# Sums on VectorE, output weights' splits two places ahead, operands kept by operand and loaded in place

## The chip, the cores and the metric

The kernel runs on one core of a Trainium2 chip. The metric is the device time of one execution in microseconds. A core has five engines with queues of their own, each working in order: TensorE (PE, matmuls), VectorE (DVE), ScalarE (ACT), GpSimd (POOL) and SyncE (SP, which here only issues DMAs). DMAs move data between device memory and on-chip memory; matmuls add into banks of their own, from which VectorE and ScalarE take the results. A queue that waits holds up everything behind it on its engine.

## The reference

With S = 2048 tokens, D = 1024, 32 heads of 32 and F = 3584, all in fp32:

```python
q, k, v = layernorm(x) @ wqkv            # phi(t) = (t + 1 if t > 0 else exp(t)) + 1e-6
kv  = sum over tokens of phi(k) v        # per head, 32 x 32
den = phi(q) . (sum of phi(k)) + 1e-6
s = ((phi(q) kv) / den) @ wo
g = silu((silu(xn @ w1) * (xn @ w3)) @ w2)      # xn = layernorm(x)
return x + s * g
```

## The kernel before

Each fp32 operand is split into a high and a low part (`split`, L79: ScalarE casts to the high part, VectorE subtracts it for the low one), and each product is three matmuls (`mm3`, L89: high x high, high x low, low x high). Large products are done by a scheme with seven block products in place of eight: the left side is used as A11, S2, S3, S1, A12, A22, S4 and the right side as B11, T2, T3, T1, B21, T4, B22, where the S and the T are sums and differences of blocks. `four_sums` (L591) makes S1 to S4 of a left operand, `sums_of` (L627) the T of a right one; both work on GpSimd.

The stages follow each other on TensorE: layernorm and transposes of x; then two halves of the tokens, each with products for k, v and q and 14 pairs of gate and up (products named like `ag`, `cu`, `du`); then the attention's output product (Segment "s", eight token groups m); then five layers B0 to B4, which multiply the hidden values with slices of w2 and add into `acc`; the last of them ends in `finish` (L1007: silu, times s, added to the output by an accumulating DMA).

Beside the pairs of a half run side jobs. `catch_up` takes one step of the first job at each block product (12 matmuls in a half): in half 0 the preparation of half 1 and the sums of w2 (`weight_sums`, L635), in half 1, in this order, denominators, `merge_wo` (L755), `divide` (L725), again denominators and divide. A job's `yield True` ends a step. Steps that are left at a half's end are run one after the other. The order of instructions on each engine is set by a scheduler with a timeline of its own, within the program's dependencies.

`merge_wo(k)` multiplies the masked kv of heads (`kvm`) with rows of wo, split as `wos`; the bank `wp` of the product is copied back over wo, and the sums of the four results are stored to `wp_d` as the attention's right operands. `divide(m, k)` loads phi(q) and the reciprocals r of a token group into a tile `qd`, multiplies, makes the four sums in it and stores it to `qs_d`. Its tiles come from a ring of three, `job_tile`, which all jobs share, and from which group 0 of the attention takes the raw tiles of its left operands too (`r0q_0`, `r2q_0`, `r4q_0`, `r6q_0`).

`use_up` (L613) stores the hidden values to `h_d` and `sums` (L619) their sums to `hs_d`; `left` (L957) reads the parts of the left operands from them, for the layers (`hiddens`) as for the attention (`queries`, from `qs_d`). A raw tile is loaded and then split into a tile X of pool `pb`. The attention's right operands are loaded as `wpr` into a ring of two (`attention_right`, L1051) and split into `wp`, which lies where the left operands of half 1 were: wp0 over A11, wp1 over S2, wp2 over S3, wp3 over S1, wp4 over A12, wp5 over A22, wp6 over S4.

Of the kernel before, what the change touches and what calls it, by code (L numbers as in the profile page):

```python
# [22 lines left out]
def tile_linear_attention_times_swiglu(  # L23
# [37 lines left out]
    nc.vector.memset(zacc, 0.0)  # L61

# [17 lines left out]
    def split(pair, src, bias=None):  # L80

        hi, lo = pair[:, 0], pair[:, 1]
        if bias is None:
            nc.scalar.copy(out=hi, in_=src)  # L84
            return nc.vector.tensor_sub(out=lo, in0=src, in1=hi.bitcast(F32))
# [505 lines left out]
    def four_sums(x1, x2, s12, s34):  # L591
# [3 lines left out]
        s1, s2 = (s12.rearrange("p (n g s) -> p n g s", n=2, s=P)[:, n] for n in range(2))  # L595
        s3, s4 = (s34.rearrange("p (n g s) -> p n g s", n=2, s=P)[:, n] for n in range(2))
        nc.gpsimd.tensor_add(out=s1, in0=a21, in1=a22)  # L597
# [3 lines left out]
        nc.gpsimd.tensor_sub(out=s4, in0=a12, in1=s2)  # L601
        yield

    def hidden(h, pair):
# [22 lines left out]
    def sums_of(b11, b12, b21, b22):  # L627

        nc.gpsimd.tensor_sub(out=b11, in0=b12, in1=b11)  # L629
# [99 lines left out]
    def divide(m, k):  # L729
# [13 lines left out]
        def steps(t):  # L743
# [5 lines left out]
            nc.gpsimd.dma_start(out=qs_d[m][:, k], in_=t)  # L749
# [5 lines left out]
    def merge_wo(k):  # L755
# [9 lines left out]
        def steps(e, t):  # L765
# [5 lines left out]
            split(kvm, f)  # L771
            for n in range(2):
# [339 lines left out]
```

## Time and profile before

| | before |
|---|---|
| runs | 2426.34, 2426.35, 2428.03 us; median 2426.35 |
| span of the profiled execution | 2428.0 us |
| TensorE busy | 2350.3 us, 97 % |
| VectorE busy | 1785.2 us, 74 % |
| ScalarE busy | 933.7 us, 38 % |
| GpSimd busy | 611.7 us, 25 % |
| DMA | 425.40 MB, mean 175 GB/s |

The profiled execution's own time is known only by its span, 2428.0 us; the slowest of the three runs took 2428.03. A busy TensorE is not TensorE at its peak: a matmul of 128x512 may follow another sooner than its recorded duration, so the count of matmuls in a stretch tells more than its busy time. In lists of waits stand the waiting engine, what it wrote and its line, what released it, and the total in us, the times and the longest. In tables by stretch stand, for each engine, the busy us and the number of instructions, then TensorE's granted clock, the DMA engines' busy share and GB/s. In groups of instructions stand line, engine, operation, written and read names, shape and count, then busy us and the mean ns of one, or three durations (least, median, most).

### The profile page before, as it was taken

What the parts mean: (1) busy time and instruction counts of PE and PEld (TensorE: products, weight loads), DVE (VectorE), ACT (ScalarE), POOL (GpSimd) and SP (SyncE); (2) the same over time, 40 slices, a digit from 0 to 9 for tenths busy, and PEclk for the clock granted to TensorE, in tenths of its full rate; (3) what the DMA queues carried; (4) which work ended last, traced back from release to release, by engine and by line L of the source; (5) the groups of instructions that cost most, each with busy time, mean ns of one, the idle gap of its engine ahead of it and who ended that gap; (6) DMA issues with size and microseconds to landing.
All of it is one profiled execution on the core that took longest, in us unless ns stands there. A gap on an engine that the chain in (4) does not pass through costs nothing.

```text
span 2428.0 us, 30795 instructions
## 1 busy us (share of the span) xinstructions
PE 2350.3 (97%) x10544; PEld 1937.2 (80%) x10544; DVE 1785.2 (74%) x2699; ACT 933.7 (38%) x1659; POOL 611.7 (25%) x848
## 2 busy tenths in 40 slices
PE   7999999999999999999889999999899999999997
PEld 5788888788888888887767888888687788888876
DVE  8655888888887765567777878887655576766786
ACT  4434544333333244354333333334323533342432
POOL 3000112356756210010333544243330000000032
PEclk9999999999999999999999999999899999999999
DMA  3211455567667641134454555457776565876698
GB/s 123 85 52 62 148 166 170 177 210 239 224 203 238 238 174 53 53 113 129 139 186 165 199 184 197 146 183 238 247 231 196 173 206 160 258 236 181 197 232 199
DMA packets 380285, 425.40 MB, mean 175 GB/s; under 512 B 20528, under 2 KB 309296, under 8 KB 380016
## 3 DMA queue, kind: packets, MB, share of 16 engines
q1 hardware_dynamic: 349600, 327.74, 43.2%
q0 software_dynamic: 30528, 95.70, 11.9%
q8 instruction: 82, 1.34, 0.2%
q14 instruction: 75, 0.61, 0.1%
HBM read 277.35 MB, written 153.35 MB: 177 GB/s over the span
## 4 chain that ended last, share of the span: by engine, by line
PE 78%; DMA 7%; DVE 7%; issue 4%; POOL 2%; ACT 1%; SPq 0%; POOLq 0%; DVEq 0%; ACTq 0%
PE cB L92 1%; PE kv L507 1%; DMA wpr<-wp_d 1%; PE dB L94 1%; PE cB L94 1%; PE dB L92 1%; PE cB L93 1%; PE dB L93 1%; PE aB L92 1%; PE aB L94 1%; PE aB L93 1%; DMA rA12B<-h_d 1%; PE den L714 1%; DVE acc L879 1%; PE trk L474 1%
## 5 line engine op out<-in xcount | busy, mean ns | idle before, releaser
L615 POOL DMA_DIRECT2D h_d<-sg x112 | 61.6, 550 | 359.2 <-DVE sg L614 354.8
L576 POOL DMA_DIRECT2D pq_d<-pq x32 | 17.4, 545 | 481.1 <-DVE pq L468 481.0
L896 POOL DMA_DIRECT2D u_d<-uB x32 | 17.3, 540 | 415.6 <-DVE uB L879 343.3
L879 DVE TENSOR_TENSOR acc<-cB,acc 128x512 f32<-128x512 f32 x50 | 34.4, 689 | 38.8 <-PE cB L94 38.8
L597 POOL TENSOR_TENSOR qd<-qd 128x128 f32<-128x128 f32 x32 | 25.2, 788 | 145.6 <-DVE qd L746 132.5
L879 DVE TENSOR_TENSOR acc<-dB,acc 128x512 f32<-128x512 f32 x56 | 38.6, 689 | 27.7 <-PE dB L94 27.5
L601 POOL TENSOR_TENSOR hs<-sg,hs 128x256 f32<-128x256 f32 x56 | 52.4, 935 | 1.6
L598 POOL TENSOR_TENSOR hs<-hs,sg 128x256 f32<-128x256 f32 x56 | 48.2, 860 | 0.0
L629 POOL TENSOR_TENSOR w<-w 128x256 f32<-128x256 f32 x28 | 26.0, 930 | 70.4 <-DMA w<-in_B_w 70.4
L600 POOL TENSOR_TENSOR hs<-sg 128x256 f32<-128x256 f32 x56 | 43.7, 781 | 0.0
L597 POOL TENSOR_TENSOR hs<-sg,sg 128x256 f32<-128x256 f32 x56 | 43.0, 768 | 1.0
L1020 POOL DMA_DIRECT2D out<-acc x28 | 24.3, 879 | 66.3 <-DVE acc L1015 61.5
L1002 POOL DMA_DIRECT2D s_d<-s x32 | 17.4, 544 | 93.5 <-DVE s L879 46.1
L84 ACT CAST XS4B<-rS4B 128x384 fp32r<-128x384 f32 (+1 forms) x40 | 19.7, 492 | 53.5 <-PE cB L94 37.4
L84 ACT CAST XA11B<-rA11B 128x384 fp32r<-128x384 f32 (+1 forms) x40 | 19.7, 492 | 50.0 <-PE dB L94 21.2
L92 PE MATMUL aB<-B,XA12B 128*128 128x512 f32 x87 | 35.2, 404 | 3.5 <-ACT XS2B L84 3.2
L92 PE MATMUL cB<-T,XA22B 128*128 128x512 f32 x87 | 34.9, 401 | 3.6 <-DVE acc L879 3.3
L84 ACT CAST XA12B<-rA12B 128x384 fp32r<-128x384 f32 (+1 forms) x40 | 19.7, 493 | 48.1 <-PE dB L94 22.5
L84 ACT CAST XA22B<-rA22B 128x384 fp32r<-128x384 f32 (+1 forms) x40 | 19.7, 492 | 43.5 <-PE aB L94 25.0
L92 PE MATMUL aB<-B,XA11B 128*128 128x512 f32 x87 | 34.2, 393 | 1.5 <-ACT XA11B L84 1.5
L84 ACT CAST XS3B<-rS3B 128x384 fp32r<-128x384 f32 (+1 forms) x40 | 19.7, 493 | 41.1 <-DMA rS3B<-hs_d 18.5
L507 PEld LDWEIGHTS kv<-kvr 128*128 128x128 f32 x256 | 33.5, 191 | 2.5
(5846 smaller groups left out, 8759.5 us busy)
## 6 DMA issues: line engine op xcount, KB each, us to landing
h_d<-sg POOLq DMA_DIRECT2D x112, 256.0 KB, 3.4
qs_d<-qd POOLq DMA_DIRECT2D x32, 512.0 KB, 3.7
hs_d<-hs POOLq DMA_DIRECT2D x60, 256.0 KB, 4.1
w<-in_B_w SPq DMA_DIRECT2D x56, 256.0 KB
wt_d<-w SPq DMA_DIRECT2D x28, 512.0 KB
hs_d<-hs SPq DMA_DIRECT2D x52, 256.0 KB
pq_d<-pq POOLq DMA_DIRECT2D x32, 256.0 KB, 3.2
a_dS<-xo SPq DMA_DIRECT2D x16, 512.0 KB
```

What stands on the lines that cost most here:

```text
L84: nc.scalar.copy(out=hi, in_=src)
L92: nc.tensor.matmul(acc, lhsT=wh, rhs=ah, start=start, stop=False, skip_group_check=True)
L93: nc.tensor.matmul(acc, lhsT=wh, rhs=al, start=False, stop=False, skip_group_check=True)
L94: nc.tensor.matmul(acc, lhsT=wl, rhs=ah, start=False, stop=stop, skip_group_check=True)
L507: nc.tensor.matmul(acc, lhsT=r[:, 1, t], rhs=r[:, 0, t], start=t == 0, stop=t == C // P - 1)
L597: nc.gpsimd.tensor_add(out=s1, in0=a21, in1=a22)
L598: nc.gpsimd.tensor_sub(out=s2, in0=s1, in1=a11)
L600: nc.gpsimd.tensor_sub(out=s3, in0=a11, in1=a21)
L601: nc.gpsimd.tensor_sub(out=s4, in0=a12, in1=s2)
L615: nc.gpsimd.dma_start(out=h_d[i][2 * h + c][:, 2 * k + n], in_=sg[n, c])
L629: nc.gpsimd.tensor_sub(out=b11, in0=b12, in1=b11)
L879: return V.tensor_add(out=c, in0=src, in1=c)
```

## The change

- `four_sums` and `sums_of` work on VectorE.
- `merge_wo` splits both halves of wo, and lets a step pass, before it multiplies them; the steps of a job grow from 3 to 5 (first of a pair) and from 7 to 10 (second). Its stores go through POOL's queue.
- The hidden values and their sums go to one tensor `ho_d`, kept by operand: all that one left operand needs of a token group lies together for each partition. A21 is not stored. `qs_d` is kept by operand too.
- The layers' left operands, and wp2 to wp6, are loaded into the low half of their split tile and split in place. The left operands of groups 1 to 7 of the attention come into the two large raw tiles.
- Pools `pb`, `pe`, `pc` end with the attention; the layers have pools of their own: `px` with 12 split left operands, `pl`, `pd`, `pu` and two for `acc`.

```diff
-    h_d = [[dram.tile([P, f1 - f0, C], F32, name=f"h_d{f0}_{c}") for c in range(NCH)] for f0, f1 in FB]
-    hs_d = [[dram.tile([P, (f1 - f0) // 2, 2, C], F32, name=f"hs_d{f0}_{c}") for c in range(NCH)] for f0, f1 in FB]
+    KEPT = ["A11", "A12", "A22", "S1", "S2", "S3", "S4"]
+    ho_d = [[dram.tile([P, NT, len(KEPT), (f1 - f0) // 2, P], F32, name=f"ho_d{f0}_{c}") for c in range(NCH)]
+            for f0, f1 in FB]
...
-    qs_d = [dram.tile([P, ND // 2, 4, 2 * P], F32, name=f"qs_d{m}") for m in range(S // (2 * P))]
+    QUERIES = ["A11", "A21", "A12", "A22", "S1", "S2", "S3", "S4"]
+    qs_d = [dram.tile([P, len(QUERIES), ND // 2, P], F32, name=f"qs_d{m}") for m in range(S // (2 * P))]
...
-    def split(pair, src, bias=None):
+    def split(pair, src=None, bias=None):
 
         hi, lo = pair[:, 0], pair[:, 1]
+        if src is None:
+            src = lo.bitcast(F32)
...
-    pb = ctx.enter_context(tc.tile_pool(name="pb", bufs=8))
-    pe = ctx.enter_context(tc.tile_pool(name="pe", bufs=3))
-    pc = ctx.enter_context(tc.tile_pool(name="pc", bufs=6))
     era1 = ExitStack()
+    pb = era1.enter_context(tc.tile_pool(name="pb", bufs=8))
+    pe = era1.enter_context(tc.tile_pool(name="pe", bufs=3))
+    pc = era1.enter_context(tc.tile_pool(name="pc", bufs=6))
...
-        s1, s2 = (s12.rearrange("p (n g s) -> p n g s", n=2, s=P)[:, n] for n in range(2))
-        s3, s4 = (s34.rearrange("p (n g s) -> p n g s", n=2, s=P)[:, n] for n in range(2))
-        nc.gpsimd.tensor_add(out=s1, in0=a21, in1=a22)
-        nc.gpsimd.tensor_sub(out=s2, in0=s1, in1=a11)
+        s1, s2 = (s12.rearrange("p (g n s) -> p g n s", n=2, s=P)[:, :, n] for n in range(2))
+        s3, s4 = (s34.rearrange("p (g n s) -> p g n s", n=2, s=P)[:, :, n] for n in range(2))
+        nc.vector.tensor_add(out=s1, in0=a21, in1=a22)
+        nc.vector.tensor_sub(out=s2, in0=s1, in1=a11)
         yield
-        nc.gpsimd.tensor_sub(out=s3, in0=a11, in1=a21)
-        nc.gpsimd.tensor_sub(out=s4, in0=a12, in1=s2)
+        nc.vector.tensor_sub(out=s3, in0=a11, in1=a21)
+        nc.vector.tensor_sub(out=s4, in0=a12, in1=s2)
...
-            nc.gpsimd.dma_start(out=h_d[i][2 * h + c][:, 2 * k + n], in_=sg[n, c])
+            halves = sg[n, c].rearrange("p (g t s) -> p g t s", t=2, s=P)
+            if n == 0:
+                nc.gpsimd.dma_start(out=ho_d[i][2 * h + c][:, :, 0, k], in_=halves[:, :, 0])
+            else:
+                nc.gpsimd.dma_start(out=ho_d[i][2 * h + c][:, :, 1:3, k], in_=halves)
...
-                queue.dma_start(out=hs_d[i][2 * h + c][:, k, e], in_=o[e])
+                queue.dma_start(out=ho_d[i][2 * h + c][:, :, 3 + 2 * e:5 + 2 * e, k],
+                                in_=o[e].rearrange("p (g n s) -> p g n s", n=2, s=P))
...
-        nc.gpsimd.tensor_sub(out=b11, in0=b12, in1=b11)
-        nc.gpsimd.tensor_sub(out=b12, in0=b22, in1=b12)
+        nc.vector.tensor_sub(out=b11, in0=b12, in1=b11)
+        nc.vector.tensor_sub(out=b12, in0=b22, in1=b12)
         yield True
-        nc.gpsimd.tensor_sub(out=b22, in0=b22, in1=b11)
-        nc.gpsimd.tensor_sub(out=b21, in0=b21, in1=b22)
+        nc.vector.tensor_sub(out=b22, in0=b22, in1=b11)
+        nc.vector.tensor_sub(out=b21, in0=b21, in1=b22)
...
-            nc.gpsimd.dma_start(out=qs_d[m][:, k], in_=t)
+            nc.gpsimd.dma_start(out=qs_d[m][:, :, k], in_=t.rearrange("p a (n s) -> p (a n) s", s=P))
...
+            o = [pb.tile([P, 2, C], FR, tag="b", name=f"wos{j}_{n}") for n in range(2)]
             for n in range(2):
-                o = pb.tile([P, 2, C], FR, tag="b", name=f"wos{j}_{n}")
-                split(o, t[:, n])
+                split(o[n], t[:, n])
                 yield True
+            yield True
+            for n in range(2):
                 acc = bank(f"wp{j}_{n}")
-                mm3(acc, (kvm[:, 0], kvm[:, 1]), (o[:, 0], o[:, 1]), True, True)
+                mm3(acc, (kvm[:, 0], kvm[:, 1]), (o[n][:, 0], o[n][:, 1]), True, True)
                 nc.scalar.copy(out=t[:, n], in_=acc)
-            yield True
+                yield True
             if e:
                 b = [t[:, n] for t in both for n in range(2)]
                 for n, i in (("B11", 0), ("B21", 2), ("B22", 3)):
                     store(n, b[i])
+                yield True
                 yield from sums_of(*b)
+                yield True
                 for n, i in (("T1", 0), ("T3", 1), ("T4", 2), ("T2", 3)):
                     store(n, b[i])
-                for _ in range(3):
+                for _ in range(2):
                     yield True
 
         def store(n, t):
             g, e = divmod(7 * k + PRODUCTS.index(n), 4)
-            nc.sync.dma_start(out=wp_d[g][:, e], in_=t)
+            nc.gpsimd.dma_start(out=wp_d[g][:, e], in_=t)
...
+        staged = None
+        for e, n in enumerate(PRODUCTS):
+            n = PARTNER[n]
+            if e % (2 if m == 0 else 4) == 0:
+                staged = (job_tile([P, 2, ND // 2, P], f"r{e}q_{m}") if m == 0 else
+                          praw.tile([P, 4, ND // 2, P], F32, tag="raw", name=f"r{e}q_{m}"))
+            raw = staged[:, e % (2 if m == 0 else 4)]
+            loads[:] = [nc.sync.dma_start(out=raw, in_=qs_d[m][:, QUERIES.index(n)])]
+            yield n, pb.tile([P, 2, ND // 2, P], FR, tag="b", name=f"X{n}q_{m}"), raw
...
-        h_ = h_d[i][m // NT].rearrange("p (k e) s -> p k e s", e=2)
-        hs = hs_d[i][m // NT]
-        return left(m, m % NT, [h_[:, :, e] for e in range(2)], [hs[:, :, e] for e in range(2)],
-                    (FB[i][1] - FB[i][0]) // 2, f"B{i}")
+        for n in PRODUCTS:
+            n = PARTNER[n]
+            t = px.tile([P, 2, (FB[i][1] - FB[i][0]) // 2, P], FR, tag="x", name=f"X{n}B{i}_{m}")
+            loads[:] = [nc.sync.dma_start(out=t[:, 1].bitcast(F32), in_=ho_d[i][m // NT][:, m % NT, KEPT.index(n)])]
+            yield n, t, None
...
-            raw = praw.tile([P, 4, C], F32, tag="raw", name=f"wpr{g}")
+            place = pa.tile([P, 4, 2, C], FR, tag=AOPS[g], name=f"wp{g}")
+            raw = praw.tile([P, 4, C], F32, tag="raw", name=f"wpr{g}") if g < 2 else None
             for i in range(2):
-                nc.sync.dma_start(out=raw[:, 2 * i:2 * i + 2], in_=wp_d[g][:, 2 * i:2 * i + 2])
-            places[g] = raw, pa.tile([P, 4, 2, C], FR, tag=AOPS[g], name=f"wp{g}")
-        return places[g][0][:, e]
+                o = slice(2 * i, 2 * i + 2)
+                nc.sync.dma_start(out=place[:, o, 1].bitcast(F32) if raw is None else raw[:, o], in_=wp_d[g][:, o])
+            places[g] = raw, place
+        return places[g][0] if places[g][0] is None else places[g][0][:, e]
...
-    pw = ctx.enter_context(tc.tile_pool(name="pw", bufs=1, reuse_waits="tile"))
+
+    def late_pool(name, bufs=1):
+        return ctx.enter_context(tc.tile_pool(name=name, bufs=bufs, reuse_waits="tile"))
+
+    pu, pacc, pl, pw, pacc2, pd, px = (late_pool(*how) for how in (
+        ("pu", 3), ("pacc",), ("pl", 6), ("pw",), ("pacc2",), ("pd", 2), ("px", 12)))
+
+    def late_small(name):
+        pool, tag = (pd, "d") if name.startswith("xs") else (pl, "c")
+        return pool.tile([P, C], F32, tag=tag, name=name)
```

ScalarE's queue at the first pair of merge_wo, before (`wos` the split wo, `kvm` the masked kv, `wp` the bank of their product, the others operands of hidden products):

```order
807 L84 CAST wos_0_9344<-wo_9243 128x512
808 L84 CAST kvm_9341<-kvf_9339 128x128
809 L84 CAST T3g_1__9365<-wg_1__9151 128x512
810 L778 COPY wo_9243<-wp_0_9368 128x512
811 L84 CAST wos_1_9373<-wo_9243 128x512
812 L84 CAST B21g_1__9390<-wg_1__9151 128x512
813 L84 CAST T2g_1__9363<-wg_1__9151 128x512
814 L778 COPY wo_9243<-wp_1_9393 128x512
815 L84 CAST kvm_9420<-kvf_9418 128x128
816 L84 CAST wos_0_9423<-wo_9337 128x512
817 L84 CAST T4g_1__9441<-wg_1__9151 128x512
818 L778 COPY wo_9337<-wp_0_9444 128x512
```

And now:

```order
806 L90 CAST kvm_9323<-kvf_9321 128x128
807 L90 CAST T1g_1__9311<-wg_1__9133 128x512
808 L90 CAST wos_0_9326<-wo_9225 128x512
809 L90 CAST T3g_1__9348<-wg_1__9133 128x512
810 L90 CAST wos_1_9327<-wo_9225 128x512
811 L90 CAST B21g_1__9367<-wg_1__9133 128x512
812 L791 COPY wo_9225<-wp_0_9388 128x512
813 L90 CAST T2g_1__9346<-wg_1__9133 128x512
814 L414 COPY ug_1__9483<-ag_1__9484 128x512
815 L90 CAST T4g_1__9408<-wg_1__9133 128x512
816 L90 CAST B22g_1__9440<-wg_1__9133 128x512
817 L791 COPY wo_9225<-wp_1_9411 128x512
```

The cast of wos_1 stood behind the copy of wp_0, the product of wos_0; now both casts stand ahead of it, and two operands of other products with them.

SP's queue around the end of the hidden products, before (`qd5_3` is the last of the jobs ahead of the attention, `r0q_0` to `r6q_0` the left operands of its group 0, `wpr` its right operands):

```order
L740 DMA qd5_3_13487<-pq_d1_2_82 128x256
...
L973 DMA r0q_0_13697<-qs_d0_145 128x4x128 x2
L1056 DMA wpr1_13741<-wp_d1_125 128x1024 x2
L973 DMA r2q_0_13706<-qs_d0_145 128x4x128 x2
L973 DMA r4q_0_13715<-qs_d0_145 128x4x128 x2
L1056 DMA wpr2_13753<-wp_d2_126 128x1024 x2
L1056 DMA wpr3_13765<-wp_d3_127 128x1024 x2
L973 DMA r6q_0_13724<-qs_d0_145 128x4x128
L1056 DMA wpr4_13777<-wp_d4_128 128x1024 x2
```

And now, where `wp6` waits for the last hidden product, each qd for the store of the tile before it in the ring, and r0q_0 for that of qd5_1:

```order
L751 DMA qd5_0_13581<-pq_d1_2_84 128x256
L1062 DMA wp6_13779<-wp_d6_112 128x2x512 x2
L749 DMA qd5_1_13640<-r_d2_137 128x1x256
...
L749 DMA qd5_2_13651<-r_d2_137 128x1x256
...
L749 DMA qd5_3_13662<-r_d2_137 128x1x256
...
L751 DMA qd5_3_13662<-pq_d1_2_84 128x256
L982 DMA r0q_0_13679<-qs_d0_127 128x512 x2
L982 DMA r2q_0_13688<-qs_d0_127 128x512 x2
L982 DMA r4q_0_13697<-qs_d0_127 128x512 x2
L982 DMA r6q_0_13706<-qs_d0_127 128x512
```

The left operands of group 0 stood among the loads of wpr, behind qd5_3 as the last job; now they stand behind all of wp and behind qd5_1 to qd5_3, which themselves come after wp6.

More of the change, by code (lines that the diff above doesn't have):

```diff
@@ L834, in tile_linear_attention_times_swiglu, with __init__ @@
     class Segment:
-        def __init__(self, name, nk, first, last, place, right, left, acc, end=None):
-            self.last, self.U = last, {}
+        def __init__(self, name, nk, first, last, place, right, left, acc, sum_of, end=None):
+            self.last, self.U, self.sum_of = last, {}, sum_of
             self.name, self.nk, self.first = name, nk, first
@@ L955, in tile_linear_attention_times_swiglu @@
     loads = []
-    def left(m, g, halves, sums, nk, name, first=False):
-        halves = [t.rearrange("p k (g t s) -> p k g t s", t=2, s=P) for t in halves]
-        sums = [t.rearrange("p k (n g s) -> p k n g s", n=2, s=P) for t in sums]
-        where = {"A11": halves[0][:, :, g, 0], "A12": halves[1][:, :, g, 0], "A22": halves[1][:, :, g, 1]}
-        for n in range(4):
-            where[f"S{n + 1}"] = sums[n // 2][:, :, n % 2, g]
-        big = None
-        for e, n in enumerate(PRODUCTS):
-            n = PARTNER[n]
-            if first:
-                if e % 2 == 0:
-                    big = job_tile([P, 2, nk, P], f"r{e}{name}_{m}")
-                t = big[:, e % 2]
-            else:
-                t = signed(f"r{n}{name}_{m}")[:, :nk * P].rearrange("p (k s) -> p k s", s=P)
-            loads[:] = [nc.sync.dma_start(out=t, in_=where[n])]
-            yield n, t
     def queries(m):
@@ L1045, in run @@
                 around(m)
-            seg.tokens(m, m == 0 or m == NG - 1 and nxt is not None, between)
+            seg.tokens(m, m == 0 or m == NG - 1 and (ends or nxt is not None), between)
     places = {}
@@ L1068, in tile_linear_attention_times_swiglu @@
         attention.right(k)
-    run(attention)
+    run(attention, ends=True)
     assert all(next(j, None) is None for j, _ in jobs)
@@ L1085, in tile_linear_attention_times_swiglu @@
         layers[0].right(k)
[L1086 removed]
+    acc.extend((pacc if m < 5 else pacc2).tile([P, 2, 2, C], F32, tag=f"acc{m}", name=f"acc{m}") for m in range(NG))
     for i, seg in enumerate(layers):
```

27 lines of the change are left out of this document (14 added, 13 removed).

## The prediction

> **What bounds the kernel now.** I read the page first. TensorE is busy nearly all the span, and the chain of work that ended last runs through it for four fifths.
>
> ```profile
> PE 2350.3 (97%) x10544; PEld 1937.2 (80%) x10544; DVE 1785.2 (74%) x2699; ACT 933.7 (38%) x1659; POOL 611.7 (25%) x848
> PE 78%; DMA 7%; DVE 7%; issue 4%; POOL 2%; ACT 1%; SPq 0%; POOLq 0%; DVEq 0%; ACTq 0%
> ```
>
> So time can only be won where TensorE is not at its rate. I find these places by stretches of 100 us: the count of matmuls in brackets behind the first number, the granted clock after the five engines.
>
> ```profile
> 400.00:500.00 100.00, 97.98 (x441) 80.50 (x440) 83.09 (x121) 42.44 (x73) 23.04 (x34) 0.98 0.51 162
> 500.00:600.00 100.00, 100.00 (x443) 82.81 (x442) 90.64 (x102) 33.80 (x57) 68.23 (x86) 1.00 0.70 230
> 1100.00:1200.00 100.00, 90.13 (x379) 71.87 (x379) 73.71 (x99) 41.97 (x75) 18.73 (x24) 0.97 0.41 134
> 1200.00:1300.00 100.00, 90.49 (x377) 71.64 (x376) 76.28 (x93) 35.09 (x65) 32.35 (x35) 0.97 0.47 154
> 1300.00:1400.00 100.00, 100.00 (x443) 82.78 (x442) 83.08 (x104) 32.02 (x54) 48.14 (x75) 1.00 0.57 193
> 1700.00:1800.00 100.00, 91.63 (x381) 72.97 (x380) 59.00 (x85) 29.20 (x50) 32.33 (x57) 0.93 0.78 244
> 1800.00:1900.00 100.00, 92.69 (x390) 73.42 (x389) 54.44 (x94) 37.72 (x76) 17.11 (x31) 0.97 0.64 204
> 2000.00:2100.00 100.00, 98.95 (x436) 81.21 (x435) 68.55 (x120) 35.95 (x68) 3.24 (x6) 1.00 0.64 198
> 2300.00:2400.00 100.00, 92.83 (x383) 73.83 (x382) 79.85 (x132) 34.76 (x69) 34.13 (x33) 0.95 0.93 230
> ```
>
> A full stretch of the wide products holds 443 matmuls, one per 0.2257 us. Matmuls missing from 443 times 0.2257 is what a stretch lost: 14.4 + 14.9 = 29.3 us in 1100 to 1300 (merge_wo), 14.0 in 1700 to 1800 (start of the attention), 12.0 in 1800 to 1900 (its end and the start of layer B0), 1.6 in 2000 to 2100, 13.5 in 2300 to 2400 (last layer); in 400 to 500, 2.0 idle and 0.02 of the clock, together some 3. The waits say on what:
>
> ```profile
> PE wp L92 <- ACT wos L84: 11.5, 8, 4.5
> PE T1s L92 <- ACT wp L84: 5.2, 1, 5.2
> PE cB L92 <- DVE acc L879: 3.3, 1, 3.3
> PE aB L92 <- ACT XS2B L84: 3.2, 2, 2.3
> PE wp L93 <- DVE wos L85: 3.2, 1, 3.2
> PE B11B L92 <- ACT B L84: 2.9, 1, 2.9
> PE wp L92 <- ACT kvm L84: 1.8, 1, 1.8
> ```
>
> **Sums on VectorE.** POOL loses its additions in four_sums and sums_of; VectorE gains them. Prices, GpSimd's and VectorE's on the same or the nearest shape:
>
> ```profile
> L601 POOL TENSOR_TENSOR hs<-sg,hs 128x256 f32<-128x256 f32 x56 | 52.4, 935 | 1.6
> L629 POOL TENSOR_TENSOR w<-w 128x256 f32<-128x256 f32 x28 | 26.0, 930 | 70.4 <-DMA w<-in_B_w 70.4
> L597 POOL TENSOR_TENSOR qd<-qd 128x128 f32<-128x128 f32 x32 | 25.2, 788 | 145.6 <-DVE qd L746 132.5 <-DMA qd<-pq_d 10.5 <-DMA hs_d<-hs 2.6
> L508 DVE TENSOR_TENSOR kvacc<-kv,kvacc 128x128 f32<-128x128 f32 x32 | 9.1, 284 | 0.0
> L85 DVE TENSOR_TENSOR XA11B<-rA11B,XA11B x40: 414/550/1650, 1839.6 to 2396.2; 128x384 fp32r<-128x384 f32 x32, 128x256 fp32r<-128x256 f32 x8
> L321 DVE TENSOR_TENSOR wu__5040<-wu__5040 128x512 f32<-128x512 f32 x4 | 7.7, 1923 | 0.1
> L321 DVE TENSOR_TENSOR wq__1786<-wq__1786 128x512 f32<-128x512 f32 x4 | 2.8, 692 | 0.1
> ```
>
> VectorE gets 56 x 4 hidden sums and 28 x 4 weight sums at 0.414 (its 128x256 price), 32 x 4 query sums at 0.284 and 16 sums of 128x512 at 0.692: 93 + 46 + 36 + 11 = 186 us. It also loses the stretching: the L321 group at 1923 ns ran beside POOL sums, the one at 692 with POOL free of them. In the fullest stretch, 500 to 600, its 102 instructions at an undisturbed 0.68 are 69 us, and the 64 sums that POOL has there add 27: 96 of 100. So VectorE is close to full there but not over it, and TensorE, with no loss there now, should stay so: cost 0, covered by queued products; if that cover is gone, it is what lies above 100. The one stall of the stretched evacuations (400 to 500) goes: **-3** (bounds -3 and 0).
>
> **merge_wo two places ahead.** Before, ScalarE's cast of the second half of wo stands behind the copy of the first product's bank, so each pair waits for itself. Now both casts come ahead of the copy, with 15 to 44 matmuls (3.4 to 9.9 us) between what the split needs and the product that reads it; a cast is 0.62 (as XA11's, below), a split or an evacuation's add 0.69, three or four in a row: under the slack. The waits (11.5 + 3.2 + 1.8 = 16.5) go, and with them most of the clock's share, 0.03 of two stretches, 6 us, and the short refills: of 29.3 I take **-25** (bounds -15, the waits nearly alone, and -29).
>
> VectorE's new wait stands here: sums_of writes over halves of wo whose stores (POOL's queue now) must have landed, 3.4 us as s_d's below, with one place, 2.7, between; four stalls of about 1 us, behind which evacuations queue, covered by the same slack: 0 (up to +3, inside the bounds above). The stores themselves (0.55 us an issue, POOL idle for three quarters), the order of the kept operands in ho_d, and A21 left out of it cost nothing that any wait shows.
>
> **The start of the attention.** merge_wo takes more places than it had (5 for 3 and 10 for 7 in a pair of jobs, 20 more over four pairs, some 54 us at 12 matmuls, 2.7 us, a place), so the division jobs behind it slip: qd4_3 and qd5_0 to qd5_3 now fall after the last hidden product. The left operands of token group 0 use the same three buffers as these jobs, and SP's order shows them behind qd5_3. Before, they were cast at 1673.8, ahead of the last hidden product.
>
> ```profile
> 1680.00:1690.00 10.00, 10.00 (x46) 8.29 (x45) 6.51 (x12) 3.44 (x7) 2.32 (x5) 1.00 0.93 279
> 1690.00:1700.00 10.00, 10.00 (x46) 8.29 (x45) 9.20 (x15) 5.91 (x12) 2.56 (x5) 1.00 0.93 291
> 1710.00:1720.00 10.00, 4.64 (x11) 2.53 (x9) 2.89 (x4) 1.20 (x3) 1.86 (x3) 0.51 0.96 294
> L973 SPq DMA_DIRECT2D r0q<-qs_d x2: 559/590/622, 1670.4 to 1671.0; - x2
> L84 ACT CAST XA11s<-r0q x1: 622/622/622, 1673.8 to 1673.8; 128x512 fp32r<-128x512 f32 x1
> qs_d<-qd POOLq DMA_DIRECT2D x2, 512.0 KB, 5.0
> L738 SPq DMA_DIRECT2D qd<-r_d x64: 517/530/926, 1257.1 to 1796.8; - x64
> L746 DVE SCALAR_TENSOR_TENSOR qd<-qd 128x512 f32<-128x512 f32 x32 | 21.8, 682 | 3.6 <-DMA qd<-pq_d 3.6
> ```
>
> Let T be the end of the last hidden product. VectorE's queue after T, in its order: c12u, three sums, two wp splits, the gate's product, more sums and splits: qd4_3's last sum at T+7, four wp5 splits, qd5_0's product, two wp6 splits and its sums to T+14; its store lands 5.0 later (the landing in this stretch), T+19. Only then qd5_3 may load (four issues of 0.53, landing 3.3 after its issue as r0q did): T+24; product and sums 0.7 + 4 x 0.28: T+26. Beside it qd5_1's last sum, T+18, its store, T+23, r0q_0's load 3.3, T+26.4, cast 0.6: **TensorE at T+27**, if no transfer queues. But they do: from wp4's load (allowed 60 matmuls, 13.5 us, ahead of T) up to r0q_0 there are five loads of wp (5.2 MB), seven of group 1 (1.8), five of qd (2.6), four stores of qs_d (2.1) and the last pair's stores (1.8), 13.5 MB; at the 285 GB/s of the full rows, 47 us: T+34, and T+36 with the cast. I take T+30. The long idle costs a half-clock stretch behind it (the row at 0.51 is one), 3 us. So 33 in place of 14.0: **+19** (bounds: +11, for T+22 at the unloaded landing of 3.7, and +25). The waits for wp (T1s, 5.2) hide under it.
>
> **The start of B0.** The weight loads of B0 go into memory of the closed pools, so the first waits for the last store of s.
>
> ```profile
> s_d<-s POOLq DMA_DIRECT2D x32, 256.0 KB, 3.4
> L990 SPq DMA_DIRECT2D rB11B<-in_B_w x2: 333/442/551, 1857.0 to 1865.1; - x2
> L84 ACT CAST B<-rB11B x1: 617/617/617, 1860.3 to 1860.3; 128x512 fp32r<-128x512 f32 x1
> ```
>
> Before, this load was out at 1857.0, ahead of the attention's end (1858.0: the 2.9 us wait for B ended with this cast). Now: evacuation 0.8, landing 3.4, load 3.3, cast 0.6: 8.1 us for 2.9, +5. Of the 12.0 lost here, 6 are neither this wait nor the clock's 3; the left operands of B0, now loaded far ahead, had a part in them, and I take 1: **+4** (bounds 0, with all 6 gone, and +8, with the store's landing doubled).
>
> **Later layers.** Left operands load in place, 12 tiles deep; before, 4 raw and 8 split tiles gave the same depth, so lookahead is unchanged. What changes is 1,536 contiguous bytes where it was 512, and no stall of the raw ring: some of the 6.5 us of waits in the last layer (cB, aB) and their clock goes, though the DMA at 0.93 stays near full. **-6** (bounds 0 and -12). The small loss at 2000: **-1** (0 to -1.6). The tail with xs loaded earlier: **-2** (0 to -3).
>
> **A rule against it.** The stores of qs_d go out in 1,024 pieces of 512 bytes where they were 128 of 4 KB.
>
> ```profile
> L749 POOL DMA_DIRECT2D qs_d<-qd x32: 531/554/573, 1317.2 to 1816.1; - x32
> ```
>
> By this row an issue is 0.55 us with 128 pieces; nothing here shows one with 1,024. Bounds: 0.55, and eight times that, 4.4. I take the lower, since no row shows a growth. The Trainium skill ("DMA: Bandwidth & Descriptors", section "Anatomy of one DMA") calls descriptor generation small and variable, so that many can be emitted before it shows, which is the first bound; the same page (section "SWDGE vs HWDGE vs iDMA") has GpSimd compute one pair for each piece, which leans to the second and would add three dearer stores to the chain, some +12 in the sum. No run here decides it.
>
> **Sum.** -3 - 25 + 19 + 4 - 6 - 1 - 2 = -14. The profiled execution's span is 2428.0 and the runs have a median of 2426.35, so the difference is set against the median: **2412 us**.
>
> **Rivals.**
> 1. The start does no more harm than before: the transfers before T run ahead, since group 0's operands are ready when the DMA queue is (before it was full too, 0.93 to 0.96). For it: VectorE is only at 0.6 to 0.9 around there, so the sums may come earlier than my count. Against: r0q_0 stands behind four stores in a chain. -33 in all: 2393.
> 2. Slower: the piecewise stores are dear (4.4 us an issue, and the rate of the rows with small pieces, 230 GB/s, in place of 285, so that the 13.5 MB take 59 us, T+46, and the three stores 4 more): TensorE at T+50, +39 at this place. Sum +6, or +12 without the last layer's gain: 2434. It decides from T+44 on, where the gain at merge_wo is eaten.
> 3. The change doesn't do what it says: TensorE still waits in merge_wo, now for wo's load or a late bank; -10 there instead of -25, sum about +1: 2427. Against: the wait named ACT's cast, not a DMA.
>
> **How the numbers follow.** A measurement of this kernel tells about 0.2 %, 5 us, from no change. Chances: the forecast 0.59 (2400 to 2424 with its own bounds), rival 1 0.17, rival 2 0.16, rival 3 0.08. Faster: 0.49 of the forecast, all of rival 1, 0.66; same: 0.08 of the forecast, 0.04 of rival 2, 0.05 of rival 3, 0.17; slower the rest, 0.17. The range takes in most of rival 1 and rival 2's point: 2388 to 2434.
>
> **What would show it.** Right: no "wp <- ACT wos" of some us in the waits; 1100 to 1300 near 440 matmuls a stretch; at the start of the attention one wait of TensorE for the cast of XA11 of group 0, of about 30 us, with r0q loaded last; at B0 a wait of 8; no POOL sums beyond the preparation, and L321 groups at 0.69. Wrong: that wait below 14 us or above 43; VectorE at 100 % with TensorE waiting in 500 to 600; qs_d issues on POOL well over 0.55 us; waits for wos as before.

## The result and the profile after

The changed kernel takes 2446.83 us (median of 4 runs, 2443.98 to 2448.69), the kernel before 2427.19 us in the same comparison: a ratio of 1.0066, 95 % interval 1.0049 to 1.0084. It is slower: the two medians differ by 19.6 us, and the ratio makes it 16 us, between 12 and 20. The forecast was 2412, 14 us faster, in a range from 2388 to 2434; the measured time lies above that range. The profiled execution has a span of 2446.7 us. All medians below are of executions in the usual state; one of e6, 2492.5 us at a lower granted clock, is left out.

First the page of the changed kernel, busy times and the chain that ended last:

```profile
PE 2337.9 (96%) x10544; PEld 1935.9 (79%) x10544; DVE 1748.3 (71%) x3181; ACT 939.0 (38%) x1659; POOL 304.2 (12%) x397
PE 84%; DMA 6%; issue 4%; DVE 3%; POOL 2%; SPq 1%; ACT 0%; POOLq 0%; ACTq 0%; DVEq 0%
```

VectorE has 482 more instructions and is busy for 37 us less: the additions that it took over cost less than what it had lost beside GpSimd, where its instructions ran longer. The sums alone do that: in e3 below VectorE is busy for 1742.4 us, with 480 more instructions than before. The same table by stretches:

```profile
500.00:600.00 100.00, 100.00 (x443) 82.81 (x442) 82.00 (x156) 34.68 (x58) 17.24 (x20) 1.00 0.67 227
1100.00:1200.00 100.00, 100.00 (x441) 82.57 (x440) 81.35 (x137) 46.91 (x82) 13.55 (x21) 1.00 0.47 154
1200.00:1300.00 100.00, 100.00 (x441) 82.45 (x440) 72.88 (x127) 39.72 (x71) 14.08 (x22) 1.00 0.44 148
1600.00:1700.00 100.00, 63.45 (x268) 51.59 (x266) 70.91 (x135) 32.74 (x58) 15.57 (x19) 0.83 0.61 207
1700.00:1800.00 100.00, 92.00 (x395) 75.95 (x396) 53.78 (x100) 26.99 (x45) 15.30 (x24) 0.93 0.66 217
1800.00:1900.00 100.00, 88.86 (x376) 71.75 (x375) 55.86 (x104) 34.35 (x67) 11.85 (x20) 0.93 0.59 203
```

At merge_wo (1100 to 1300) 2 matmuls are missing in each stretch, 0.9 us in all, where 29.3 us were lost before. From 1600 to 1800, 175 and 48 are missing: 39.5 + 10.8 = 50.3 us at the attention's start, in place of 14.0. At the start of B0 it is 15.1 us, in place of 12.0. The waits of TensorE (total us, how many, the longest) name the places:

```profile
PE B11s L98 <- ACT XA11q L90: 39.9, 1, 39.9
PE cB L98 <- DVE acc L894: 11.7, 5, 3.8
PE B11B L98 <- ACT B L90: 11.6, 2, 10.2
PE cu__13517 L98 <- DVE c22u__13544 L437: 4.6, 1, 4.6
PE dB L98 <- DVE acc L894: 3.1, 2, 2.7
```

One wait of 39.9 us for the left operand of the attention's group 0 is the loss. It ends at 1708.0, so the last hidden product ended at T = 1668.1. The chain of the changed kernel ahead of that, in rows of its timeline (start, us, what):

```profile
1676.13 0.86 POOL L760 DMA_DIRECT2D qs_d<-qd  x1 [0.57 <-DVE qd L607]
...
1684.38 0.84 SPq L749 DMA_DIRECT2D qd<-r_d  x1
...
1687.89 1.40 SPq L751 DMA_DIRECT2D qd<-pq_d  x1
...
1696.29 0.69 DVE L757 SCALAR_TENSOR_TENSOR qd<-qd 128x512 f32<-128x512 f32 x1 [3.26 <-DMA qd<-pq_d]
1696.90 0.28 DVE L607 TENSOR_TENSOR qd<-qd 128x128 f32<-128x128 f32 x1
...
1697.48 0.85 POOL L760 DMA_DIRECT2D qs_d<-qd  x1 [7.01 <-DVE qd L603]
...
1704.24 0.80 SPq L982 DMA_DIRECT2D r0q<-qs_d  x2
...
1707.33 0.63 ACT XA11q L90
1708.00 0.80 PE B11s L98
```

Read it from the top. The store of qd4_3 is issued at 1676.1 and has landed at 1683.7; only then do the four loads of qd5_2 leave, and their data are there at 1696.2, 11.8 us after the first issue. VectorE works in order, and the last sum of qd5_1 stands behind qd5_2's product: it runs at 1696.9, its store is issued at 1697.5 and has landed at 1704.2, and r0q is issued right behind that. Cast and matmul follow. The chain that the profile infers goes through a load of qd5_3 instead, which stands before r0q in SP's queue; but the four loads of qd5_3 had been issued by 1698.2, and then SP waited 6.0 us for the store. qd5_3 is not on the path.

Meanwhile the DMA engines fell from full to less than half, and TensorE's clock stood at a half:

```profile
1670.00:1680.00 10.00, 0.00 (x0) 0.00 (x0) 8.91 (x21) 3.48 (x7) 6.04 (x7) 0.61 0.99 349
1690.00:1700.00 10.00, 0.00 (x0) 0.00 (x0) 3.39 (x10) 0.00 (x0) 1.32 (x2) 0.50 0.40 137
```

The second new loss is in the last layer. From the first to the last of its 504 matmuls (504 x 0.2257 is 113.8 us; I count 503 steps, 113.5), before and after:

```profile
2290.50:2418.50 128.00, 120.82 (x504) 96.68 (x504) 103.44 (x172) 45.98 (x89) 39.65 (x40) 0.96 0.92 227
```

```profile
2300.10:2437.30 137.20, 121.04 (x505) 96.66 (x503) 105.79 (x171) 46.20 (x87) 39.25 (x40) 0.96 0.83 210
```

It lost 14.5 us and now loses 23.7, though the DMA engines are less busy, 0.83 for 0.92.

### The profile page after: what moved, and what is told of

It is laid out like the page before. It is cut to its first block, busy times and chain, and to the rows that moved or that the text cites. A ratio compares the mean times of both kernels' runs of the same rounds, so it can differ in the third digit from the quotient of the medians.

```text
span 2446.7 us, 30779 instructions
## 1 busy us (share of the span) xinstructions
PE 2337.9 (96%) x10544; PEld 1935.9 (79%) x10544; DVE 1748.3 (71%) x3181; ACT 939.0 (38%) x1659; POOL 304.2 (12%) x397
## 3 DMA queue, kind: packets, MB, share of 16 engines
q0 software_dynamic: 30976, 95.71, 11.3%
## 4 chain that ended last, share of the span: by engine, by line
PE 84%; DMA 6%; issue 4%; DVE 3%; POOL 2%; SPq 1%; ACT 0%; POOLq 0%; ACTq 0%; DVEq 0%
PE cB L98 1%; PE cB L99 1%; PE cB L100 1%; PE dB L98 1%; PE dB L100 1%; PE dB L99 1%; PE aB L98 1%; PE aB L100 1%; PE aB L99 1%; PE kv L513 1%; DMA XA11B<-ho_d 1%; PE bB L98 1%; DMA qd<-pq_d 1%; PE bB L99 1%; PE bB L100 1%
## 5 line engine op out<-in xcount | busy, mean ns | idle before, releaser
L625 POOL DMA_DIRECT2D ho_d<-sg x56 | 51.2, 915 | 552.3 <-DVE sg L620 452.1
L633 POOL DMA_DIRECT2D ho_d<-hs x60 | 54.6, 909 | 41.3 <-DVE hs L604 29.2
L623 POOL DMA_DIRECT2D ho_d<-sg x56 | 37.8, 674 | 102.5 <-DVE sg L620 96.1
L98 PE MATMUL cB<-T,XA22B 128*128 128x512 f32 x87 | 36.1, 415 | 11.7 <-DVE acc L894 11.7
L760 POOL DMA_DIRECT2D qs_d<-qd x32 | 27.7, 869 | 134.1 <-DVE qd L607 64.5
L98 PE MATMUL B11s<-wp,XA11q 128*128 128x512 f32 x8 | 4.2, 530 | 39.9 <-ACT XA11q L90 39.9
L91 DVE TENSOR_TENSOR XS3B<-XS3B 128x384 fp32r<-128x384 f32 (+1 forms) x40 | 22.2, 556 | 25.8 <-ACT XS3B L90 25.5
L91 DVE TENSOR_TENSOR XA11B<-XA11B 128x384 fp32r<-128x384 f32 (+1 forms) x40 | 21.2, 529 | 25.5 <-ACT XA11B L90 25.5
L91 DVE TENSOR_TENSOR XS1B<-XS1B 128x384 fp32r<-128x384 f32 (+1 forms) x40 | 21.1, 529 | 25.0 <-ACT XS1B L90 24.9
L98 PE MATMUL dB<-B,XS4B 128*128 128x512 f32 x87 | 34.6, 398 | 3.1 <-DVE acc L894 3.1
L91 DVE TENSOR_TENSOR XS2B<-XS2B 128x384 fp32r<-128x384 f32 (+1 forms) x40 | 21.3, 533 | 20.9 <-ACT XS2B L90 20.8
L757 DVE SCALAR_TENSOR_TENSOR qd<-qd 128x512 f32<-128x512 f32 x32 | 21.9, 683 | 18.8 <-DMA qd<-pq_d 18.8
L99 PE MATMUL cB<-T,XA22B 128*128 128x512 f32 x87 | 35.3, 405 | 0.0
```

The lines of the kernel that those rows point to most:

```text
L98: nc.tensor.matmul(acc, lhsT=wh, rhs=ah, start=start, stop=False, skip_group_check=True)
L99: nc.tensor.matmul(acc, lhsT=wh, rhs=al, start=False, stop=False, skip_group_check=True)
L623: nc.gpsimd.dma_start(out=ho_d[i][2 * h + c][:, :, 0, k], in_=halves[:, :, 0])
L625: nc.gpsimd.dma_start(out=ho_d[i][2 * h + c][:, :, 1:3, k], in_=halves)
L633: queue.dma_start(out=ho_d[i][2 * h + c][:, :, 3 + 2 * e:5 + 2 * e, k], in_=o[e].rearrange("p (g n s) -> p g n s", n=2, s=P))
L757: nc.vector.scalar_tensor_tensor(t[:, :2], t[:, :2], 1e-6, t[:, 2:], op0=ALU.add, op1=ALU.mult)
```

## The experiments

All ratios are to the kernel before, run on the same chip, which there had medians from 2429.8 to 2431.6 us.

**e1, ten steps.** The gap, the step before the sums and the trailing steps of merge_wo are taken out, five steps a pair, its early splits stay (an excerpt):

```diff
                 split(o[n], t[:, n])
                 yield True
-            yield True
             for n in range(2):
...
                     store(n, b[i])
-                yield True
                 yield from sums_of(*b)
                 yield True
...
-                for _ in range(2):
-                    yield True
```

> The changed kernel, but merge_wo's jobs take 4 and 6 steps (10 for a pair, as before the change; the changed kernel has 15), with both halves of wo still split ahead of their products. Theory (the longer merge_wo pushes the last divisions behind the hidden products, and the left operands of the attention's group 0 wait for their ring): TensorE's wait for XA11q of 39.9 us and the half clock behind it go, the loss in 1600 to 1800 falls from 50 us to at most 14 as in the kernel before, total 2405 to 2415. Rival (the wait comes from loading wp in place of hidden operands, which frees them late): the loss stays over 40 us, total 2440 or more. At merge_wo itself at most 5 us come back.

Measured: 2399.9 us, ratio 0.9875 (0.9853 to 0.9897). The same stretches of e1:

```profile
1100.00:1200.00 100.00, 99.75 (x438) 81.94 (x437) 79.68 (x138) 47.07 (x84) 15.68 (x25) 1.00 0.49 164
1600.00:1700.00 100.00, 99.92 (x441) 82.43 (x440) 83.32 (x158) 44.37 (x77) 19.01 (x26) 1.00 0.76 260
1700.00:1800.00 100.00, 100.00 (x443) 82.81 (x442) 56.79 (x112) 27.42 (x51) 17.43 (x28) 1.00 0.66 224
```

The start of the attention loses 0.5 us instead of 50.3, with wp still loaded in place, and merge_wo loses 2.3 us for 0.9. So the five steps a pair are the cause of the loss, and they bought 1.4 us: one place ahead was nearly enough. The total is 5 us below the theory's range, since so little was left of the wait.

**e2, group 0 without the ring.** With the 15 steps, `queries(0)` loads into the split tile instead of a tile of the ring:

```diff
+            if m == 0:
+                t = pb.tile([P, 2, ND // 2, P], FR, tag="b", name=f"X{n}q_{m}")
+                loads[:] = [nc.sync.dma_start(out=t[:, 1].bitcast(F32), in_=qs_d[m][:, QUERIES.index(n)])]
+                yield n, t, None
+                continue
...
```

> The changed kernel with its 15 steps, but the left operands of the attention's group 0 are loaded into their split tiles and not into the ring of three that the divisions use. Theory (the ring joins the operands to the chain of division stores): the wait for XA11q falls from 39.9 us to under 10, TensorE then waits for wp as in the kernel before, loss in 1600 to 1800 between 14 and 25 us, total 2410 to 2422. Rival (the transfers between the last allowed load and the first product set it, 13.5 MB): the wait moves to wp or XA11q at some 30 us, total 2437 or more.

Measured: 2413.2 us, 0.9929 (0.9903 to 0.9955). The wait for XA11q is gone; from 1600 to 1800 TensorE loses 20.6 us, and its longest waits are for evacuations, for c22u and for wp:

```profile
PE cs L98 <- DVE s L901: 6.0, 3, 4.0
PE cu__13517 L98 <- DVE c22u__13544 L437: 4.5, 1, 4.5
PE T2s L98 <- ACT wp L90: 2.7, 1, 2.7
```

Both ends of the mechanism are shown: the divisions come late (e1), and the ring hands their lateness on (e2).

**e3, only the sums** in the kernel before, all eight additions of four_sums and sums_of as this one:

```diff
-        nc.gpsimd.tensor_add(out=s1, in0=a21, in1=a22)
+        nc.vector.tensor_add(out=s1, in0=a21, in1=a22)
```

> The kernel before with only the sums moved to VectorE (four_sums and sums_of). Theory (VectorE loses the stretching beside GpSimd that it pays with the added work): the 3.7 us in 400 to 500 go, and a part of the 29 us at merge_wo, total 2415 to 2423, VectorE at 82 to 96 per cent in 500 to 600. Rival (VectorE is too full, or its waits for loads hold evacuations up): TensorE loses time in 500 to 700 or 1300 to 1700, total 2427 to 2440.

Measured: 2413.4 us, 0.9930 (0.9908 to 0.9952). Its stretches:

```profile
500.00:600.00 100.00, 100.00 (x443) 82.81 (x442) 81.88 (x156) 34.57 (x58) 10.55 (x20) 1.00 0.70 234
1100.00:1200.00 100.00, 92.75 (x401) 74.35 (x400) 73.65 (x125) 44.02 (x79) 7.04 (x13) 1.00 0.44 144
1200.00:1300.00 100.00, 95.14 (x411) 76.20 (x409) 74.16 (x134) 37.13 (x68) 4.86 (x9) 1.00 0.57 188
```

The loss at merge_wo falls from 29.3 to 9.5 + 7.2 = 16.7 us by the sums alone, 12.6 us less. The profiled execution, 2404.2 us, is the fastest of the five, so that figure is on the high side. Nothing is lost in 500 to 600, where VectorE is at 82 %. The total is 1.6 us below the theory's range.

**e4, only merge_wo** as changed, in the kernel before; the edit is that part of the diff above, from `o = [pb.tile` to the store through POOL's queue.

> The kernel before with only merge_wo as changed (two places ahead, 15 steps a pair, stores on POOL's queue); sums on GpSimd, operands and pools as before. Theory (the steps alone make the divisions late): 25 to 29 us gained in 1100 to 1300 and 30 to 45 lost at the attention's start, total 2427 to 2445. Rival (the late divisions cost only together with loads in place): no loss at the start beyond the 14 us of before, total 2397 to 2402.

Measured: 2437.5 us, 1.0032 (1.0019 to 1.0045). Merge_wo loses 1.6 us: the early splits alone win 27.7 of the 29.3. The attention's start loses 50.6 us for 14.0 and shows the same wait, with sums on GpSimd and wp not loaded in place:

```profile
PE B11s L92 <- ACT XA11s L84: 36.3, 1, 36.3
```

A second wait, 7.6 us for c22u, is there too; VectorE stands then before the product of a division whose load has not landed.

**e5, only operands kept by operand, loads in place and pools**: the changed kernel with sums and merge_wo of before.

> The changed kernel with the sums back on GpSimd and merge_wo as before: what is left is operands kept by operand, loads in place and the pools. Theory (the last layer's 9 us more and the later start of B0 come from these, the rest of the change has no part in them): last layer 22 to 26 us over its 504 matmuls (14.5 before), start of B0 4 to 7 us later, the attention's start not worse than the 14 us of before; total 2424 to 2436. Rival (the last layer suffers from VectorE's or the stores' new load): the last layer stays at 11 to 15 us and the total at 2412 to 2424.

Measured: 2422.5 us, 0.9968 (0.9956 to 0.9980), 1.5 us under the theory's range. The last layer is the theory's:

```profile
2276.10:2413.10 137.00, 120.34 (x504) 95.86 (x503) 107.31 (x172) 46.45 (x88) 39.34 (x40) 0.98 0.83 211
```

That is 23.5 us over 113.5; in e3 and e4, with the old layers, it is 11.3 and 12.9. The gain in total is for the most part at the attention's start, 5.4 us lost for 14.0. Loading wp in place is one candidate for that; the operands of groups 1 to 7, which get large raw tiles, changed with it, and the two were not separated. The start of B0 loses 15.6 us for 12.0.

**e6, ss by POOL**, on e1:

```diff
-        nc.sync.dma_start(out=ss, in_=s_d[2 * m + t][:, cols])
+        nc.gpsimd.dma_start(out=ss, in_=s_d[2 * m + t][:, cols])
```

> The ten-step kernel (e1) with the last layer's loads of s (ss) issued by POOL instead of SP. Theory (SP's queue stands behind ss, which waits for VectorE's multiplication with ss of a group and a half before, so the left operands behind it are issued a few us ahead of their use): the left operands' loads run ahead, the last layer's loss falls from 25 to 10 to 15 us, total 2383 to 2390. Rival (the DMA engines are full there, share 0.89): the loss stays over 20 us and the total at 2393 or more.

Measured: 2398.3 us, 0.9873 (0.9857 to 0.9890), as e1; the last layer loses 21.1 us for 24.9. SP standing behind ss is a small part at most. My theory fell.

**e7, more room for ss**, on e1:

```diff
-        ("pu", 3), ("pacc",), ("pl", 6), ("pw",), ("pacc2",), ("pd", 2), ("px", 12)))
+        ("pu", 3), ("pacc",), ("pl", 8), ("pw",), ("pacc2",), ("pd", 2), ("px", 10)))
```

> The ten-step kernel (e1) with 8 in place of 6 tiles for ss, and 10 in place of 12 for the left operands. Theory (the ring of ss holds SP up, not the depth of the left operands): last layer's loss down from 25 to 10 to 18 us, total 2384 to 2392. Rivals: the depth of the left operands counts, loss 27 us or more; the DMA engines are full, no change within 3 us.

Measured: 2394.1 us, 0.9853 (0.9838 to 0.9868). Last layer 16.9 us: better, but B2 and B3 lose 7.1 us for 2.2 in e1. Partly right, and no settlement.

**e8, pl first**, on e1:

```diff
-    pu, pacc, pl, pw, pacc2, pd, px = (late_pool(*how) for how in (
+    pl, pu, pacc, pw, pacc2, pd, px = (late_pool(*how) for how in (
-        ("pu", 3), ("pacc",), ("pl", 6), ("pw",), ("pacc2",), ("pd", 2), ("px", 12)))
+        ("pl", 6), ("pu", 3), ("pacc",), ("pw",), ("pacc2",), ("pd", 2), ("px", 12)))
```

> The ten-step kernel (e1) with the pool of the layers' small tiles (pl) in front of the others, so that it lies in other memory of the closed pools; the first weight load of B0 then waits for a product of the last attention group and not for the last store of s. Theory (that store's landing is what makes B0 late): TensorE's wait at B0's start falls from 9.4 to 2 to 5 us, half-clock time behind it shrinks, total 4 to 10 us less than e1. Rival (the loads themselves, seven raw weights behind twelve left operands, are the wait): within 2 us of e1.

Measured: 2389.6 us, 0.9835 (0.9818 to 0.9852). At the start of B0, e1 has one wait of 9.4 us for the first weight, e8 two shorter ones:

```profile
PE T2B L98 <- ACT T L90: 3.4, 1, 3.4
PE B22B L98 <- ACT B L90: 2.7, 1, 2.7
```

The first weight's load leaves at 1808.0 in e8 and at 1817.0 in e1, where SP had waited 4.9 us for a store of s. So the landing of the last store of s did make B0 late. Which closed pool a new one lies over is worth some 10 us here: 7.7 at the start of B0 (16.3 to 8.6 lost) and 2.6 in the last layer (24.9 to 22.3). The two waits sum to 6.1 us, a little over the theory's 2 to 5.

**e9, raw tiles again**, on e8: `("pr", 4)` is added behind `pl`, `px` has 8 tiles, and `hiddens` loads into a raw tile (the part in `hiddens`):

```diff
-            t = px.tile([P, 2, (FB[i][1] - FB[i][0]) // 2, P], FR, tag="x", name=f"X{n}B{i}_{m}")
-            loads[:] = [nc.sync.dma_start(out=t[:, 1].bitcast(F32), in_=ho_d[i][m // NT][:, m % NT, KEPT.index(n)])]
-            yield n, t, None
+            nk = (FB[i][1] - FB[i][0]) // 2
+            raw = pr.tile([P, C], F32, tag="r", name=f"r{n}B{i}_{m}")[:, :nk * P].rearrange("p (k s) -> p k s", s=P)
+            loads[:] = [nc.sync.dma_start(out=raw, in_=ho_d[i][m // NT][:, m % NT, KEPT.index(n)])]
+            yield n, px.tile([P, 2, nk, P], FR, tag="x", name=f"X{n}B{i}_{m}"), raw
```

> The kernel of e8 (ten steps, pl first), but the layers' left operands come into a ring of 4 raw tiles and are split from there into 8 tiles, as in the kernel before; they still lie by operand in memory. Theory (loading in place is what slows the last layer: SP's queue then waits for TensorE's release of an operand tile, with ss and u behind it, and the loads come out just in time): last layer's loss 15 us or less (22.3 in e8), total 2378 to 2384. Rival (storing by operand, or the new pools' rings): the loss stays at 20 to 25 us, total 2387 or more.

Measured: 2376.4 us, 0.9770 (0.9754 to 0.9786), the fastest of all. Its last layer:

```profile
2242.90:2363.70 120.80, 116.91 (x504) 95.06 (x503) 103.80 (x173) 46.24 (x90) 39.82 (x40) 0.99 0.91 236
```

7.3 us lost, against 22.3 in e8: the raw tiles are worth 15 us here. It is also less than the 14.5 of the kernel before; storing by operand may be the reason, but the pools differ too, and that was not separated. The total is 1.6 us below the theory's range. Over the last layer ScalarE's casts of the operands S4 and S1 wait for their loads thus, in the changed kernel and then in e9:

```profile
ACT XS4B L90 <- DMA XS4B<-ho_d: 11.9, 6, 3.7
ACT XS1B L90 <- DMA XS1B<-ho_d: 13.7, 5, 4.1
```

```profile
ACT XS4B L90 <- DMA rS4B<-ho_d: 4.6, 3, 2.0
ACT XS1B L90 <- DMA rS1B<-ho_d: 14.9, 5, 3.5
```

S4 shows the largest change, S1 almost none; over all seven operands these waits fall from 57.8 to 45.0 us. TensorE's wait for evacuations, which was 11.7 us in the changed kernel, is short:

```profile
PE cB L98 <- DVE acc L890: 2.1, 1, 2.1
```

**e10, whole pieces**: the changed kernel with qs_d laid out as before, so that its stores have 128 pieces of 4 KB (an excerpt; the declaration of qs_d and its loads change with it):

```diff
-            nc.gpsimd.dma_start(out=qs_d[m][:, :, k], in_=t.rearrange("p a (n s) -> p (a n) s", s=P))
+            nc.gpsimd.dma_start(out=qs_d[m][:, k], in_=t)
```

> The changed kernel, with qs_d laid out as before: its stores go out in 128 pieces of 4 KB instead of 1,024 of 512 bytes. Theory (the pieces make the stores in the chain of divisions land later, 6.4 us against 3.9 in the kernel before): the wait for XA11q falls from 39.9 us by 2 to 9 us (one to three stores of 2 to 3 us), total 2438 to 2445. Rival (the landing is late since the DMA engines are busy, whatever the pieces): landing 6 us or more and the wait within 1.5 us of 39.9.

Measured: 2444.1 us, 1.0051 (1.0034 to 1.0069), the wait 37.1 us. Issues on POOL of the changed kernel and of e10:

```profile
L760 POOL DMA_DIRECT2D qs_d<-qd x32: 841/864/1021, 1344.1 to 1819.9; - x32
```

```profile
L760 POOL DMA_DIRECT2D qs_d<-qd x32: 532/551/580, 1344.5 to 1817.0; - x32
```

And the landing in this stretch, 1640 to 1720, of the changed kernel and of e10:

```profile
qs_d<-qd POOLq DMA_DIRECT2D x8, 512.0 KB, 6.5
```

```profile
qs_d<-qd POOLq DMA_DIRECT2D x8, 512.0 KB, 6.9
```

896 more pieces cost 0.31 us of issue. In this stretch the landing is no faster with whole pieces; over all 32 stores its median is 3.8 us for 4.3, and 0.3 of that is the issue. The wait moved by 2.8 us, so the number fell in the theory's range, but not by its mechanism: the landing is late with whole pieces too. VectorE's order differs as well, since in e10 the last sum of qd5_1 stands ahead of qd5_2's product. What makes up the 2.8 us stays open.

**e11, both rings of e7 and the pool order of e8.**

> The kernel of e8 with 8 tiles for ss and the weights and 10 for the left operands, as in e7. Theory: the gain at B0 (e8) and that in the last layer (e7, 8 us) add up, total 2381 to 2386. Rival (the shallower left operands cost in B0 and B1 what the last layer gains): 2387 or more.

Measured: 2388.5 us, 0.9824 (0.9805 to 0.9843): 1.2 us from e8, the rival's value. The last layer loses 18.3 us for 22.3, B2 and B3 7.2 for 2.5.

**e12, 8 tiles in place**, on e8: the pool px has 8 in place of 12, nothing else changes.

> The kernel of e8 with 8 in place of 12 split tiles for the layers' left operands, still loaded in place: e9's depth without its raw tiles. Theory (in place, a load can start only when TensorE lets the tile go, and its cast and split stand next in the queues, so that VectorE waits for the transfer with evacuations behind): last layer's loss 20 us or more (22.3 in e8, 7.3 in e9), total 2386 or more. Rival (the splits stand too far ahead of their use, 12 deep): loss 15 us or less, total 2376 to 2382.

Measured: 2406.6 us, 0.9898 (0.9876 to 0.9920). The last layer is the slowest of all:

```profile
2252.40:2393.40 141.00, 124.54 (x505) 96.64 (x503) 110.00 (x174) 48.18 (x92) 38.61 (x39) 0.95 0.82 210
```

27.5 us lost. With e9's 8 split tiles but no raw tiles it is 20 us worse than e9 in the last layer. Against e8, with 12 tiles, it loses 5.2 us more there, and in B2 and B3 together 12.0 us for 2.4. So the depth counts when operands are loaded in place; but at 12 places in all (e8, and e9 with 4 raw and 8 split tiles) as well as at 8 split tiles (e12 and e9) the raw tiles win, by 15 and by 20 us.

## Why the prediction was wrong

**merge_wo**: right, 29.3 to 0.9 us, -28.4 where -25 was forecast. The credit was right too: the early splits alone win 27.7 us (e4). The sums alone win some 12.6 (e3), of the same loss, so the two do not add.

**Sums**: right that TensorE loses nothing by them; the stall in 400 to 500 went. The load of VectorE in 500 to 600 was put at 96 and is 82. The step that failed is adding up durations: in the changed kernel four splits of 0.69 take 2.49 us together, since one begins before the record of the last ends. At some 0.60 us a split the 96 comes down most of the way, by estimate.

**The start of the attention**: the right place, the right wait (XA11q, released by the cast, r0q loaded last), the wrong size: +36.3 against +19, over the upper bound of +25. The step that failed is the sizing of the chain behind T, the end of the last hidden product: T+27 without queues, T+30 taken, T+39.9 measured (T is 1668.1). Its start was right, qd4_3's last sum at T+7.5 for T+7, and so was its end, 3.1 us for r0q and 0.6 for the cast. Between them qd5_1's last sum was put at T+18 and ran at T+28.8. The store of qd4_3 landed after 7.5 us, not 5.0; the four transfers of qd5_2, which waited for it, took 11.8 us to their data, not 4.9; and qd5_1's last sum stood behind qd5_2's product. Then qd5_1's own store took 6.7 us, not 5.0. qd5_0's product, put at about T+10, came at T+16.6: its last piece, issued at 1670.1, landed at 1684.3. The loads of qd5_0 to qd5_3 took 16.4, 14.1, 11.8 and 6.8 us, the six stores there 5.6 to 7.5, median 6.4. I had taken the durations of a quieter stretch for each link. The other way to the sum, all bytes at the full rate, is not the answer either: from 1690 to 1700 the engines stood at 0.40, while the chain waited for one transfer after the other. Why single transfers took so long there stays open. (The bytes give T+34, and with the cast about T+34.5; I wrote T+36.)

The rest of the 50.3 us is a stall that I did not have, and the clock. TensorE waited 4.6 us for c22u ahead of T. In the changed kernel VectorE stood 5.2 us before a split of wp loaded in place; but e4, where wp is not in place, has a stall of 7.6 us there, behind a division's product, and e1 and e5, with wp in place and without the 15 steps, have none. So it goes with the late divisions, and not with loading in place alone. The half clock cost 2.7 us behind this stall and 2.5 behind the long wait: 39.9, 4.6 and 5.2 make 49.7.

Rival 2 named this side and the place, but with another mechanism, dear pieces: e10 refutes it, with a wait of 37.1 us in whole pieces. (Its "the three stores 4 more" does not follow from 4.4 us an issue either: that is 3.85 above the 0.55 of whole pieces, 11.6 for three.) What the Trainium skill ("DMA: Bandwidth & Descriptors", section "Anatomy of one DMA") says of descriptor generation, small and variable, agrees: 0.55 to 0.86 us for eight times the pieces.

**B0**: +4 forecast; 12.0 to 15.1 in its stretch and 1.1 in the next: +4.2, and e8 shows the wait for the last store of s as the cause.

**The last layer**: forecast -6, measured +9.2. The step that failed is "lookahead is unchanged", 12 tiles for 4 and 8. By the program, a raw tile is free as soon as it is split, and its load can leave before TensorE has released the tile of the operand; in place, the load waits for TensorE, and its cast and split stand next in their queues, with evacuations behind (PE cB <- DVE acc: 11.7 us, 3.3 before, 2.1 in e9). That giving up the raw tiles is the cause is shown by e5, e9 and e12, which take them away and put them back. The way by which they act is argued in part: VectorE waits for the casts of these operands for 25.0 us in the changed kernel and 15.9 in e9, but for 23.4 in the kernel before, so these waits alone do not tell the three apart. Which of the two queues costs more was not separated.

**The tail**: -2 forecast; 9.5 and 9.4 us from the last matmul on, no change.

The measured terms, -3 - 28.4 + 36.3 + 4.2 + 9.2, make +18.3; the spans differ by 18.7. The -1 forecast for later is not in that sum: the 1.6 us at 2000 went, but 1.4 at 1500 to 1600 and 2.3 at 2100 to 2200 are new.

## What to carry to other kernels

A step added to a job that runs beside the main work is paid by whoever comes behind that job: count the steps, and see whose buffers the last jobs hold when the main work ends. A chain of load, sum and store through a small ring costs its latencies one after the other once nothing covers it, here some 7 to 16 us for the four transfers of a load and 6 to 7 for a store. Size such a chain by the durations of its own stretch, and look for the link that stands behind another in an engine's order. Loading in place saves memory, but it ties the load to the last reader of the tile; where the engine that splits is also the one that empties the banks, try raw tiles, which were worth 15 us in the last layer here.

## What the runs showed of the hardware

TensorE's granted clock was 0.50 from about 1672 on (the row of 1670 to 1680 has 0.61, that of 1690 to 1700 0.50), through the idle time, and for 5.1 us after TensorE began again at 1708.0. A stall of 40 us cost only some 2.5 us more by the clock than its length; the stall of 4.6 us (the rows from 1650 to 1670 have 0.93 and 0.73) cost 2.7, nearly the same. Stores of 512 KB from GpSimd landed after 6.4 us (median of six) at the attention's start, where 4.3 is the median of all such stores in the changed kernel and 3.7 before. The busy share of the DMA engines alone does not tell this: from 1340 to 1440, with the engines at 0.57, eight such stores landed after 4.1 us; from 1680 to 1720, at 0.58, four took 6.3. Why is open.
